# Two-problem grouped-query attention on one core: later wq pieces issued by ScalarE in another shape, first loads and x transposes in another order

## The chip, the cores and the metric

The kernel runs on one core of one Trainium2 chip. The metric is the device time of one execution in microseconds (us), the median of three runs. The engines are TensorE (PE in profiles; PEld is its weight load), VectorE (DVE), ScalarE (ACT), GpSimd (POOL) and SyncE (SP, which here only issues transfers). Transfers are issued on SyncE's queue or on ScalarE's queue and are carried out by 16 DMA engines.

## The reference

Two independent problems, A and B, of the same shapes; their outputs are set side by side. All data is bf16.

```python
B, Sq, D = 16, 80, 576
Hq, Hkv, Sk, Dh = 32, 16, 512, 128
q = (x @ wq).reshape(B, Sq, Hq, Dh).transpose(0, 2, 1, 3)
k = jnp.repeat(k_cache, Hq // Hkv, axis=1)
v = jnp.repeat(v_cache, Hq // Hkv, axis=1)
scores = jnp.einsum("bhqd,bhkd->bhqk", q, k) * (Dh ** -0.5)
p = softmax(scores, axis=-1)
o = jnp.einsum("bhqk,bhkd->bhqd", p, v)
out = o.transpose(0, 2, 1, 3).reshape(B, Sq, Hq * Dh) @ wo
# result: concatenate([out_A, out_B], axis=-1)
```

## The kernel before

**Units.** The attention is cut into 128 units U, 64 for each problem. A unit is one batch row and four K/V heads (eight query heads). Eight units in a row share one slice of wq (1024 columns, eight heads) and one half of the batch rows (8 rows of 80 queries); that group of eight is `goct`, 16 in all. For each pair of slices q the kernel goes through half 0 with both slices, then half 1 with both, so a slice is read by two `goct` (for instance 0 and 2). For each pair of slices there is then a share of the output projection.

**Work of a unit.** Four score tiles of 128 rows (one for each K/V head, 128 of its 160 query rows) and a fifth that packs the four rests of 32 rows. For a tile: QK on TensorE (L713, and L699 for the packed fifth, which takes two units at a time from the third unit on: `GRP`, `GR`); the negated row maximum on VectorE (L722); the exponential with its row sum on ScalarE (L726); a reciprocal on VectorE (L732); the scaling on GpSimd (L735); a transpose of P on TensorE (L741), copied out of PSUM by VectorE (L748, L750), or for some units' fifth tile by a DMA transpose (L754, units chosen by `RSEL`); P times V on TensorE (L788), copied out by ScalarE (L804). QK runs 13 tiles (`LA`) ahead of the rest.

**Projections.** `qp` (L589) multiplies xT by a slice of wq, for one head i of the slice and one half c of the eight rows; its result is scaled and copied to qT by ScalarE (L600) or VectorE (L601). `op` (L841) is the output projection, out of oT and wo. Problem A's x is loaded and transposed by TensorE (L507, copied out at L511); problem B's x comes by DMA transposes (`ldxt`, L527), five for each half.

**Loads.** K of a unit (L663, a DMA transpose into one of 5 slots) and x, wq, wo and the stores (L875) stand on SyncE's queue. V (L667) stands there for units 0 to 3 and on ScalarE's queue from unit 4 on. wq has two slots, one for even and one for odd slices. Slices 0 and 1 of problem A are loaded at the start, in two halves of 512 columns each (names w00, w01, w10, w11 in `FIRST`; x00 to x11 are x's parts, k0.. and v0.. the first K and V). Later slices (`goct` 4, 5, 8, 9, 12, 13) are loaded in four pieces and a rest of 64 rows (L560, L563).

**Order.** The program of every engine is an order worked out at build time by `_Sched.arrange`. Each operation has an engine (or a choice of engines), a stream, a key that sorts it within its stream, and a duration. At each step the planner takes the engine that can start first and gives it the operation of least key among the heads of its streams. Transfers get a landing time from a cost model (`dma_end`) or, for the first loads, from the table `LAND`. `after` holds a transfer back in the plan until a given P-times-V step; on the chip only real dependencies are waited for, by semaphores. Within a queue operations go in the planned order, and an operation that waits holds up what is behind it.

**What the change touches.** `FIRST`, `LATER` and `LAND` (order and landing of first loads); `WENG` (who issues later wq pieces), `WQR` and `WQX` (when: units after `sp_`, the start of the second pass of the projection that last reads the slot), `XR` (when each of the ten DMA transposes of x goes: first step and distance, in units, relative to the first projection that reads it, for half 0 and half 1); the wq pieces' shape at L556; the dependencies of `qp` on them at L607.

Of the kernel before, what the change touches and what calls it, by code (L numbers as in the profile page):

```python
# [13 lines left out]
LA = 13  # L14
# [9 lines left out]
VK = 8.0  # L24
KK = 8.0
DLAT = 0.6
XC = 0.4
QL2 = 10.3
VC = 1.75
WQC = 3.1  # L30
# [6 lines left out]
NWARM = 8  # L37
NWARM2 = 2
QP1 = (0.4, 1.1)
FIRST = ("x00", "w00", "x01", "w01", "k0", "w10", "k1", "v0", "k2", "k3", "v1", "w11", "k4")  # L40
LATER = dict(x10=-0.40, x11=-0.39, v2=-0.38, v3=-0.37)
LAND = dict(x00=4.1, w00=6.4, x01=8.0, w01=9.6, k0=11.5, w10=14.6, k1=18.1, v0=19.4, k2=21.8, k3=23.7, v1=26.4, w11=28.1,
            k4=30.3, k5=33.0, x10=35.7, x11=36.9, v2=38.0, v3=39.5, k6=43.2, k7=46.8)
NFK = 5
PTX = (0,)
NPX = 128
QEV = {160: dict(act=0.21, dve=0.24), 320: dict(act=0.32, dve=0.40), 480: dict(act=0.43, dve=0.57)}
NWC = 4
BANKS = dict(S=(0, 1, 2, 6), T=(3, 4), O=(5, 7), M=(7, 5), M0=(7, 5, 6, 3, 4), M1=(7, 6), ML=(7, 5, 6, 0, 1))
# [1 line left out]
VENG = "act"  # L51
VDUR = 0.42
VN = 1
# [6 lines left out]
XM = dict(wo=6.0, wq=6.0, wqb=6.0, RT=4.0, V=2.0, K=2.0, x=3.0)  # L60
VAF = (None, None, None, None)
STENG = "sp"
WENG = "sp"
WOENG = "sp"
WLAG = 2.0
NVS = 4
# [21 lines left out]
LPS = 1.1  # L88
LPC = 29.0
WOR = (((4.0, 1.5), (12.0, 1.5)), ((7.0, 1.6), (15.6, 1.6)), ((8.0, 1.7), (16.0, 1.7)), ((9.0, 1.7), (16.0, 1.4)))  # L90
WQR = (2.0,3.5,9.5)
WQX = {9: (5.0, 2.0), 13: (4.0, 2.0)}
XR = ((-12.0, 1.9), (-9.5, 1.6))

MM0 = 0.0025
MM1 = 1.0 / 2400.0
# [274 lines left out]
def bass_concat_heads__gqa_block_cached__gqa_block_cached__near_ridge_kernel(  # L371
# [27 lines left out]
    with ExitStack() as es:  # L399
# [6 lines left out]
        kT = sb("kT", [128, NK, 4, 512], BF16)  # L406
# [24 lines left out]
        S = _Sched()  # L431

        def R(res, ver):
            return (res, ver)
# [33 lines left out]
        def em_warmend(e):  # L468
# [5 lines left out]
              stream="warmset")  # L474
# [12 lines left out]
        for half in range(NPP):  # L487
            x_ap = probs[0][0]
            for part, (k0, k1) in enumerate(XP):
                def em_ldx(e, x_ap=x_ap, half=half, k0=k0, k1=k1):  # L490
                    src = x_ap.rearrange("b s d -> (b s) d")[half * NROW + k0 * 128:half * NROW + k1 * 128, :]
                    return e.dma_start(xs[:, half * NRT + k0:half * NRT + k1, 0:D],
                                       src.rearrange("(k p) d -> p k d", p=128))

                S.add("sp", FIRST.index("x%d%d" % (half, part)) - 100.0 if half == 0 else LATER["x%d%d" % (half, part)], em_ldx,
                      writes=[R(("xs", half * NRT + k_), 0) for k_ in range(k0, k1)], dsem="d_x%d%d" % (half, part), land=LAND["x%d%d" % (half, part)],
                      name="ldx%d.%d" % (half, part), stream="later" if half else "first", dur=0.5, cost=XC * (k1 - k0))
            for blk in range(NRT):
                rb = half * NRT + blk
                vb = S.bank("M0" if half == 0 else "M1")  # L500
                x = (XA + 0.5 * blk if blk < 2 else XA + XB + 0.1 * blk) if half == 0 else XH + 0.8 * blk

                def em_xtr(e, rb=rb, vb=vb):
                    last = None
                    for ck in range(5):
                        c0 = ck * 128 if ck < 4 else D - 128
                        last = e.transpose(psb[:, vb.phys, ck * 128:(ck + 1) * 128], xs[:, rb, c0:c0 + 128], ident[:])  # L507
                    return last

                def em_xev(e, en=None, half=half, blk=blk, vb=vb):  # L510
                    return (e.copy if en == "act" or half == 0 and blk in (1, 3) else e.tensor_copy)(xT[:, half, :, blk * 128:(blk + 1) * 128],  # L511
                                         psb[:, vb.phys, 0:640].rearrange("p (c n) -> p c n", c=5))

                S.add("pe", x, em_xtr, reads=[R(("xs", rb), 0), IDENT], writes=[R(vb, 0)], name="xtr%d" % rb,
                      stream="X", dur=_mm(5, 128), lat=0.2, alloc=[vb])
                S.add(("act", "dve") if half else "act" if blk in (1, 3) else "dve", x + 0.3, em_xev, reads=[R(vb, 0)], writes=[R(("xT", half, blk), 0)],
                      name="xev%d" % rb, stream="xed" if half else "xea" if rb in (1, 3) else "xev",
                      dur=dict(act=0.52, dve=0.40), lat=0.13)

        for half in range(NPP):  # L520
            x_ap = probs[1][0]
            st0 = UPR + 16 * half - lead[NG // 2 + 2 * half]
            for ck in range(5):
                def em_ldxt(e, x_ap=x_ap, half=half, ck=ck):
# [6 lines left out]
                      writes=[R(("xT", half, b_), 1) for b_ in range(NRT)] if ck == 0 else [R(("xT", half, "t", ck), 1)],  # L531
# [7 lines left out]
        for goct in range(NG):  # L539
            prob, q, half = unit(goct)  # L540
            wq_ap = probs[prob][3]
            wv = prob * NOCT + q
# [2 lines left out]
            pieces = () if half else ((0, 512), (512, 1024)) if goct < 2 else ((0, 1024),)  # L545
            for pi, (c0, c1) in enumerate(pieces):
                st0 = u0 - lead[goct]
                t_ld = 5.0 * st0 - 20.0 if goct > 1 else FIRST.index("w%d%d" % (goct, pi)) - 100.0
                dsem = "d_wq%d" % wsl
                eng = "sp" if goct < 2 else WENG  # L550
                strm = "first" if goct < 2 else "wq"
                sp_ = st0 if goct < 2 else u0 - 16 - lead[goct - 2] + max(QSH, lead[goct - 2] - QS0)
                if goct < 2:
                    parts = ((4, 5, c0, c1), (0, 4, c0, c1))
                else:
                    parts = tuple((0, 4, 256 * j, 256 * j + 256) for j in range(4)) + ((4, 5, 0, 1024),)  # L556
                for j, (k0, k1, n0, n1) in enumerate(parts):
                    def em_ldw(e, wq_ap=wq_ap, q=q, wsl=wsl, n0=n0, n1=n1, k0=k0, k1=k1):
                        if k0 == 4:
                            return e.dma_start(wq_sb[64:128, wsl, 4, n0:n1],  # L560
                                               wq_ap[512:576, q * 1024 + n0:q * 1024 + n1])
                        src = wq_ap[k0 * 128:k1 * 128, q * 1024 + n0:q * 1024 + n1]
                        return e.dma_start(wq_sb[:, wsl, k0:k1, n0:n1], src.rearrange("(c p) n -> p c n", p=128))  # L563

                    at = WQR[0] + WQR[1] * j + WQX.get(goct, (0.0, 0.0))[0] if k0 == 0 else WQR[2] + WQX.get(goct, (0.0, 0.0))[1]
                    S.add("act" if not goct + pi + j else eng, t_ld + 0.01 * j if goct < 2 else 5.0 * (sp_ + at), em_ldw,
                          writes=[R(("wq", wsl, k0 // 4, p_), wv) for p_ in range(n0 // 256, n1 // 256)],
                          dsem="d_we%d_%d_%d" % (goct, pi, j) if goct < 2 else "%s_%d" % (dsem, j),
                          name="ldw%d.%d.%d.%d" % (goct, pi, k0, n0), stream="wqa" if not goct + pi + j else strm if goct < 2 or k0 == 0 else "wqb", dur=0.5,
                          cost=(0.12 + 0.8 * WQC if k0 < 4 else 0.4) * (n1 - n0) / 1024.0 * (1.0 if goct < 2 or k0 else 1.25),  # L570
                          after=int(4 * (sp_ + at)) if goct > 1 else None,
                          lag=WLAG if goct > 1 else 0.0,
                          land=LAND["w%d%d" % (goct, pi)] if goct < 2 else 0.0)

            for i in range(8):
                for c in range(2):
# [77 lines left out]
        for U in range(NSU):  # L654
# [10 lines left out]
            def em_ldv(e, vc_ap=vc_ap, b=b, q=q, vs=vs):  # L665
                src = vc_ap[b:b + VN, 4 * q:4 * q + 4, :, :].rearrange("b g (p j) d -> p b g (j d)", j=4)
                return e.dma_start(v_sb[:, vs:vs + VN, :, :], src)  # L667

            S.add("sp", FIRST.index("k%d" % U) - 100.0 if U < NFK else 5.0 * gfirst[U] + 0.5 * (U - gfirst[U]) - LA - KK, em_ldk, writes=[R(("kT", ks), U)],
                  dsem="d_k%d" % ks, name="ldk%d" % U, stream="K" if U >= NFK else "first", dur=1.8, cost=KC, xp=True,  # L670
                  after=4 * U - KPH if U >= KU0 else None, lag=KLAG if U >= KU0 else 0.0, land=LAND.get("k%d" % U, 0.0))
            if U % VN == 0:
                S.add(VENG if U >= NVS else "sp", FIRST.index("v%d" % U) - 100.0 if U < 2 else LATER["v%d" % U] if U < NVS else 5.0 * U - VK, em_ldv, writes=[R(("V", vs + i_), U + i_) for i_ in range(VN)],
                      dsem="d_v%d" % vs, name="ldv%d" % U, stream="V" if U >= NVS else "later" if U > 1 else "first", dur=VDUR, cost=VN * VC,
                      lag=VLAG if U >= NVS else 0.0, after=VAF[U] if U < 4 else 4 * U - VPH if U >= VU0 else None,
                      land=LAND.get("v%d" % U, 0.0))

            vo = None
            rdma = any(a_ <= U < b_ and U % 4 in m_ for a_, b_, m_ in RSEL)
            for k in range(5):  # L680
# [274 lines left out]
```

## Time and profile before

| what | value |
|---|---|
| median of three runs | 765.19 us (764.51 to 765.31) |
| the profiled execution, its own time | 765.12 us |
| its span | 763.4 us |
| time around the span | 1.72 us |
| HBM read and written | 87.46 MB and 2.95 MB |
| DMA moved, mean | 172.86 MB, 226 GB/s |
| TensorE idle after 740 us, output projection's tail | 2.6 us of 23.4 |

The profile is of one execution. Its page begins with the busy time of each engine, then cuts the span in 40 equal slices (each digit is the busy share of a slice in tenths, 9 is 90% or more) and lists the DMA queues and the chain of work that ended last. The trace behind it answers finer questions: the timeline of one engine in a window, the busy time of all engines in a stretch, the issues of transfers with the time to landing. Ends of matmuls are modelled, so an interval between two starts says more than the idle time in brackets. "L713" is a line of the kernel; a letter q behind an engine (SPq, ACTq) marks the issuing of a transfer by it.

Transfers by issuing line, as the page has them: V on ScalarE's queue, 124 of 512 KB, 5.1 us from issue to landing; K on SyncE's queue, 128, 6.8 to 7.0 us; transposes of P, 94, 4.9 us; later wq pieces, 24 of 256 KB (5.0 to 5.2 us) and 6 of 128 KB, on SyncE's queue; wo, 32 of 288 KB; transposes of x, 10, 4.7 us.

### The profile page before, as it was taken

To read this page: it belongs to the slowest core of one execution; us is meant where nothing else is said; L and a number is where in the kernel's file an instruction comes from. 1 tells how busy PE (TensorE), PEld (TensorE's weight loads), DVE (VectorE), ACT (ScalarE), POOL (GpSimd) and SP (SyncE) were. 2 spreads that over 40 slices of the span, in tenths; PEclk is the share of its full clock that TensorE was granted. 3 is DMA by queue.
4 is the path that set the end of the run, shared out by engine and by line. 5 is a ranking of instruction groups with operands and counts; after the bars stand their busy time and mean duration, and the time that the engine had idled before them with its cause. 6 is when DMAs were issued, how large, how long until landed. Compare 5 with 4: busy or idle time off the path is not lost.

```text
span 763.4 us, 21017 instructions
## 1 busy us (share of the span) xinstructions
PE 756.6 (99%) x7876; PEld 572.3 (75%) x7876; DVE 676.7 (89%) x1602; ACT 603.7 (79%) x1691; POOL 432.3 (57%) x647
## 2 busy tenths in 40 slices
PE   8999999999999999999999999999999999999998
PEld 4677777777777777777777777777777777777786
DVE  5999999998888898999989999889889989999982
ACT  3878988888888887787887878887888888877860
POOL 1646755656565565565656555655656565564660
PEclk9999999999999999999999999999999999999999
DMA  9999999999998999999999999999999999999751
GB/s 223 261 244 240 244 248 262 233 222 234 196 240 198 255 258 251 261 218 210 241 228 214 226 248 247 240 251 251 234 219 214 199 227 237 226 264 258 182 121 32
DMA packets 431364, 172.86 MB, mean 226 GB/s; under 512 B 327968, under 2 KB 430880, under 8 KB 431264
## 3 DMA queue, kind: packets, MB, share of 16 engines
q1 hardware_dynamic: 365712, 106.43, 78.4%
q10 hardware_dynamic: 65552, 65.09, 28.4%
q8 instruction: 64, 1.05, 0.6%
q14 instruction: 36, 0.29, 0.1%
HBM read 87.46 MB, written 2.95 MB: 118 GB/s over the span
## 4 chain that ended last, share of the span: by engine, by line
PE 97%; DVE 1%; ACT 1%; issue 0%
PE ps L589 23%; PE ps L841 21%; PE ps L788 18%; PE ps L741 16%; PE ps L713 14%; PE ps L699 5%; DVE negmax L722 1%; PE ps L461 0%; ACT p_sb L726 0%; PE ps L507 0%; DVE qT L601 0%; DVE xT L511 0%; ACT qT L600 0%; ACT xT L511 0%; DVE pT L750 0%
## 5 line engine op out<-in xcount | busy, mean ns | idle before, releaser
L735 POOL TENSOR_SCALAR p_sb<-p_sb,rinv 128x512 bf16<-128x512 bf16 x640 | 429.9, 692 | 308.9 <-DVE rinv L732 308.8
L726 ACT ACTIVATE p_sb<-ps,negmax 128x512 bf16<-128x512 f32 x640 | 440.9, 695 | 90.8 <-DVE negmax L722 81.4
L722 DVE TENSOR_REDUCE negmax<-ps 128x1 f32<-128x512 f32 x640 | 425.1, 680 | 17.0 <-PE ps L713 12.2
L788 PE MATMUL ps<-pT,v_sb 128*128 128x160 bf16 x2048 | 221.9, 233 | 0.0
L750 DVE COPY pT<-ps 128x512 bf16<-128x512 bf16 x512 | 206.1, 414 | 11.9 <-PE ps L741 11.2
L589 PE MATMUL ps<-xT,wq_sb 128*128 128x320 bf16 (+2 forms) x1280 | 213.5, 299 | 1.6 <-ACT xT L511 0.7
L741 PE MATMUL ps<-ident,p_sb 128*128 128x128 bf16 x2184 | 209.8, 219 | 0.0
L788 PEld LDWEIGHTS ps<-pT,v_sb 128*128 128x128 bf16 x2048 | 164.6, 98 | 47.7 <-issue 2.1
L713 PE MATMUL ps<-kT,qT 128*128 128x512 bf16 x512 | 193.4, 379 | 0.0
L741 PEld LDWEIGHTS ps<-ident,p_sb 128*128 128x128 bf16 x2184 | 155.1, 98 | 34.4 <-issue 5.1
L841 PE MATMUL ps<-wo_sb,oT 128*128 128x288 bf16 x1280 | 170.0, 286 | 0.0
L589 PEld LDWEIGHTS ps<-xT,wq_sb 128*128 128x128 bf16 x1280 | 116.0, 98 | 52.7 <-DVE qT L601 2.5
L841 PEld LDWEIGHTS ps<-wo_sb,oT 128*128 128x128 bf16 x1280 | 122.4, 98 | 34.6 <-issue 1.7
L804 ACT CAST oT<-ps 128x320 bf16<-128x320 f32 x256 | 109.0, 426 | 29.5 <-PE ps L788 27.9
L726 ACT ACTIVATION_READ_ACCUMULATOR p_sb<-ps,negmax 128x1 f32 x640 | 132.1, 206 | 0.0
L601 DVE TENSOR_SCALAR qT<-ps 128x320 bf16<-128x320 f32 (+2 forms) x158 | 76.5, 485 | 13.8 <-PE ps L589 11.1
L600 ACT ACTIVATE qT<-ps 128x320 bf16<-128x320 f32 x98 | 43.1, 440 | 15.6 <-PE ps L589 15.4
L713 PEld LDWEIGHTS ps<-kT,qT 128*128 128x128 bf16 x512 | 50.0, 98 | 2.8 <-issue 0.2
L732 DVE RECIPROCAL rinv<-rowsum 128x1 f32<-128x1 f32 (+2 forms) x222 | 36.3, 165 | 8.2 <-ACT p_sb L726 8.2
L869 DVE TENSOR_TENSOR osb<-ps,acc 128x288 bf16<-128x288 f32 x40 | 18.3, 457 | 27.1 <-PE ps L841 27.1
L699 PE MATMUL ps<-kT,qT 128*32 128x512 bf16 x512 | 39.6, 384 | 1.0 <-ACT oT L804 0.6
L853 ACT COPY acc<-ps 128x288 f32<-128x288 f32 x40 | 15.9, 397 | 2.9 <-PE ps L841 2.7
(19 smaller groups left out, 46.3 us busy)
## 6 DMA issues: line engine op xcount, KB each, us to landing
v_sb<-in_B_v_cache_dram ACTq DMA_DIRECT2D x64, 512.0 KB, 5.1
v_sb<-in_A_v_cache_dram ACTq DMA_DIRECT2D x60, 512.0 KB, 5.1
wo_sb<-in_A_wo_dram SPq DMA_DIRECT2D x16, 288.0 KB, 5.3
wo_sb<-in_B_wo_dram SPq DMA_DIRECT2D x16, 288.0 KB, 4.6
wq_sb<-in_B_wq_dram SPq DMA_DIRECT2D x16, 256.0 KB, 5.2
out_dram<-osb SPq DMA_DIRECT2D x40, 72.0 KB, 3.4
wq_sb<-in_A_wq_dram SPq DMA_DIRECT2D x4, 512.0 KB, 5.1
v_sb<-in_A_v_cache_dram SPq DMA_DIRECT2D x4, 512.0 KB, 5.4
```

Of the source, the lines that this page charges most:

```text
L589: last = e.matmul(ps[:, vb.phys, 0:n1 - n0], lhsT=wq_sb[:, wsl, ck, i * 128:(i + 1) * 128], rhs=xT[:, half, ck, n0:n1], start=(ck == 0), s ...
L601: return e.tensor_scalar(dst, src, SCALE, None, op0=AluOpType.mult)
L699: last = e.matmul(ps[32 * g4:32 * g4 + 32, vb_.phys, :], lhsT=qT[:, qp_, g4 * 160 + 128:g4 * 160 + 160], rhs=kT[:, ks_, :, g4 * 128:(g4 + ...
L713: return e.matmul(ps[:, vb.phys, :], lhsT=qT[:, qp, gl * 160:gl * 160 + 128], rhs=kT[:, ks, :, gl * 128:(gl + 1) * 128], start=True, stop= ...
L722: return e.tensor_reduce(negmax[:, si:si + 1], ps[:, vb.phys, :], axis=AX.X, op=AluOpType.max, negate=True)
L726: return e.activation(p_sb[:, psl, :], ps[:, vb.phys, :], AF.Exp, bias=negmax[:, si:si + 1], scale=1.0, accum_out=rowsum[:, ss, k:k + 1])
L735: return e.tensor_scalar(p_sb[:, psl, :], p_sb[:, psl, :], rinv[:, ss, k:k + 1], 1.0, op0=AluOpType.mult, op1=AluOpType.mult)
L741: last = e.transpose(psb[:, vt.phys, j * 128:(j + 1) * 128], p_sb[:, psl, j * 128:(j + 1) * 128], ident[:])
L750: return cp(pT[:, pts, :, 0:4, gl * 32:gl * 32 + 32], psb[:, vt.phys, 0:512].rearrange("p (j h c) -> p j h c", j=4, h=4))
L788: last = e.matmul(ps[:, vo.phys, off:off + 160], lhsT=v_sb[:, vs, gl, j * 128:(j + 1) * 128], rhs=pT[:, pts, j, :, gl * 32:gl * 32 + 32], ...
L804: return e.copy(dst, src)
L841: last = e.matmul(ps[:, vb.phys, 0:DC], lhsT=oT[:, hi, rb * 128:(rb + 1) * 128], rhs=wo_sb[:, hi, c3 * DC:(c3 + 1) * DC], start=(hi == 0), ...
```

## The change

The second half of the second wq slice (w11) leaves its place ahead of K 4 and goes behind K 4, K 5, V 2 and x's second half; V 2 goes ahead of x. These loads now form one stream with the first ones. The later wq pieces, and their rest of 64 rows, are issued by ScalarE. A piece has 256 rows and 512 columns instead of 512 rows and 256 columns, its time in units after `sp_` is 5, 7, 10, 12.5 and, for the rest, 9.5 (before 2, 5.5, 9, 12.5 and 9.5), and the extra delays for `goct` 9 go, while those for `goct` 13 become 2 and 2. A projection depends on both pieces of its columns and on the rest. The DMA transposes of x are 1.7 units apart for half 0 (before 1.9) and, for half 1, begin 12 units ahead instead of 9.5. `NPY = 0` makes the new option `PTY` empty, so the copies of transposed P are chosen as before. The planner's landing and cost figures change.

```diff
-FIRST = ("x00", "w00", "x01", "w01", "k0", "w10", "k1", "v0", "k2", "k3", "v1", "w11", "k4")
-LATER = dict(x10=-0.40, x11=-0.39, v2=-0.38, v3=-0.37)
-LAND = dict(x00=4.1, w00=6.4, x01=8.0, w01=9.6, k0=11.5, w10=14.6, k1=18.1, v0=19.4, k2=21.8, k3=23.7, v1=26.4, w11=28.1,
-            k4=30.3, k5=33.0, x10=35.7, x11=36.9, v2=38.0, v3=39.5, k6=43.2, k7=46.8)
+FIRST = ("x00", "w00", "x01", "w01", "k0", "w10", "k1", "v0", "k2", "k3", "v1", "k4")
+LATER = ("v2", "x10", "x11", "w11", "v3")
+FKEY = dict([(n_, i_ - 100.0) for i_, n_ in enumerate(FIRST)] + [(n_, 0.05 * i_ - 0.49) for i_, n_ in enumerate(LATER)])
+LAND = dict(x00=4.1, w00=6.4, x01=8.0, w01=9.6, k0=11.5, w10=14.5, k1=18.0, v0=19.3, k2=21.8, k3=23.7, v1=26.4, k4=28.7,
+            k5=31.4, v2=33.2, x10=34.4, x11=36.0, w11=37.7, v3=39.4, k6=43.2, k7=46.5)
...
-NPX = 128
+PTY = (1,)
+NPY = 0
...
-WENG = "sp"
+WENG = "act"
...
-WQR = (2.0,3.5,9.5)
-WQX = {9: (5.0, 2.0), 13: (4.0, 2.0)}
-XR = ((-12.0, 1.9), (-9.5, 1.6))
+WQR = (5.0, 7.0, 10.0, 12.5, 9.5)
+WQX = {13: (2.0, 2.0)}
+XR = ((-12.0, 1.7), (-12.0, 1.6))
...
-                    parts = tuple((0, 4, 256 * j, 256 * j + 256) for j in range(4)) + ((4, 5, 0, 1024),)
+                    parts = tuple((2 * (j % 2), 2 * (j % 2) + 2, 512 * (j // 2), 512 * (j // 2) + 512) for j in range(4)) + ((4, 5, 0, 1024),)
...
-                    at = WQR[0] + WQR[1] * j + WQX.get(goct, (0.0, 0.0))[0] if k0 == 0 else WQR[2] + WQX.get(goct, (0.0, 0.0))[1]
+                    at = WQR[j] + WQX.get(goct, (0.0, 0.0))[k0 // 4]
...
-                          writes=[R(("wq", wsl, k0 // 4, p_), wv) for p_ in range(n0 // 256, n1 // 256)],
+                          writes=[R(("wq", wsl, w_, p_), wv) for w_ in range(k0 // 2, (k1 + 1) // 2) for p_ in range(n0 // 256, n1 // 256)],
...
-                          name="ldw%d.%d.%d.%d" % (goct, pi, k0, n0), stream="wqa" if not goct + pi + j else strm if goct < 2 or k0 == 0 else "wqb", dur=0.5,
-                          cost=(0.12 + 0.8 * WQC if k0 < 4 else 0.4) * (n1 - n0) / 1024.0 * (1.0 if goct < 2 or k0 else 1.25),
+                          name="ldw%d.%d.%d.%d" % (goct, pi, k0, n0), stream="wqa" if not goct + pi + j else strm if goct < 2 or k0 < 4 else "wqb", dur=0.5,
+                          cost=((0.12 + 0.8 * WQC) * (k1 - k0) / 4.0 if k0 < 4 else 0.4) * (n1 - n0) / 1024.0 * (1.0 if goct < 2 or k0 == 4 else 1.1),
...
-                          reads=[R(("wq", wsl, w_, i // 2), wv) for w_ in range(2)] + [R(("wqz",), 0)] + xr,
+                          reads=[R(("wq", wsl, w_, i // 2), wv) for w_ in range(3)] + [R(("wqz",), 0)] + xr,
...
-                    free_ = k in PTX and U < NPX
+                    free_ = k in PTX or k in PTY and U < NPY
```

The remaining lines of the diff replace the old look-ups in `FIRST` and `LATER` by `FKEY`, and put all first loads of SyncE into one stream ("first").

More of the change, by code (lines that the diff above doesn't have):

```diff
@@ L493, in em_ldx @@
                                        src.rearrange("(k p) d -> p k d", p=128))
-                S.add("sp", FIRST.index("x%d%d" % (half, part)) - 100.0 if half == 0 else LATER["x%d%d" % (half, part)], em_ldx,
+                S.add("sp", FKEY["x%d%d" % (half, part)], em_ldx,
                       writes=[R(("xs", half * NRT + k_), 0) for k_ in range(k0, k1)], dsem="d_x%d%d" % (half, part), land=LAND["x%d%d" % (half, part)],
-                      name="ldx%d.%d" % (half, part), stream="later" if half else "first", dur=0.5, cost=XC * (k1 - k0))
+                      name="ldx%d.%d" % (half, part), stream="first", dur=0.5, cost=XC * (k1 - k0))
             for blk in range(NRT):
@@ L547, in bass_concat_heads__gqa_block_cached__gqa_block_cached__near_ridge_kernel @@
                 st0 = u0 - lead[goct]
-                t_ld = 5.0 * st0 - 20.0 if goct > 1 else FIRST.index("w%d%d" % (goct, pi)) - 100.0
+                t_ld = 5.0 * st0 - 20.0 if goct > 1 else FKEY["w%d%d" % (goct, pi)]
                 dsem = "d_wq%d" % wsl
@@ L667, in em_ldv @@
                 return e.dma_start(v_sb[:, vs:vs + VN, :, :], src)
-            S.add("sp", FIRST.index("k%d" % U) - 100.0 if U < NFK else 5.0 * gfirst[U] + 0.5 * (U - gfirst[U]) - LA - KK, em_ldk, writes=[R(("kT", ks), U)],
+            S.add("sp", FKEY["k%d" % U] if U < NFK else 5.0 * gfirst[U] + 0.5 * (U - gfirst[U]) - LA - KK, em_ldk, writes=[R(("kT", ks), U)],
                   dsem="d_k%d" % ks, name="ldk%d" % U, stream="K" if U >= NFK else "first", dur=1.8, cost=KC, xp=True,
@@ L672, in bass_concat_heads__gqa_block_cached__gqa_block_cached__near_ridge_kernel @@
             if U % VN == 0:
-                S.add(VENG if U >= NVS else "sp", FIRST.index("v%d" % U) - 100.0 if U < 2 else LATER["v%d" % U] if U < NVS else 5.0 * U - VK, em_ldv, writes=[R(("V", vs + i_), U + i_) for i_ in range(VN)],
-                      dsem="d_v%d" % vs, name="ldv%d" % U, stream="V" if U >= NVS else "later" if U > 1 else "first", dur=VDUR, cost=VN * VC,
+                S.add(VENG if U >= NVS else "sp", FKEY["v%d" % U] if U < NVS else 5.0 * U - VK, em_ldv, writes=[R(("V", vs + i_), U + i_) for i_ in range(VN)],
+                      dsem="d_v%d" % vs, name="ldv%d" % U, stream="V" if U >= NVS else "first", dur=VDUR, cost=VN * VC,
                       lag=VLAG if U >= NVS else 0.0, after=VAF[U] if U < 4 else 4 * U - VPH if U >= VU0 else None,
```

## The prediction

> **What bounds the kernel now.** First the page's first two parts, for the share of each engine and how evenly it lies over the span.
>
> ```profile
> span 763.4 us, 21017 instructions
> PE 756.6 (99%) x7876; PEld 572.3 (75%) x7876; DVE 676.7 (89%) x1602; ACT 603.7 (79%) x1691; POOL 432.3 (57%) x647
> PE   8999999999999999999999999999999999999998
> PEclk9999999999999999999999999999999999999999
> DMA  9999999999998999999999999999999999999751
> q1 hardware_dynamic: 365712, 106.43, 78.4%
> q10 hardware_dynamic: 65552, 65.09, 28.4%
> PE 97%; DVE 1%; ACT 1%; issue 0%
> ```
>
> TensorE is busy in every slice at the full granted clock and makes 97% of the chain that ended last. The change alters no matmul, transpose or eviction in number or size. So it can win only what TensorE loses between its instructions, and it can lose without such a limit. DMA is also full: its two queues (q1 is SyncE's, q10 ScalarE's) together make 106.8% of the engines' time, which is more than 100% because packets of both overlap. Transfers that are late are therefore the place to look.
>
> Next, TensorE's own timeline at the two places where it lost most after the first 15 us:
>
> ```profile
> 32.58 0.44 PE L788 MATMUL ps<-pT,v_sb 128*128 128x160 bf16 x4
> 33.60 0.61 PE L699 MATMUL ps<-kT,qT 128*32 128x512 bf16 x8 [0.59 <-ACT oT L804]
> ...
> 406.90 0.84 PE L589 MATMUL ps<-xT,wq_sb 128*128 128x320 bf16 x5
> 408.12 0.61 PE L699 MATMUL ps<-kT,qT 128*32 128x512 bf16 x8 [0.38 <-issue]
> ```
>
> Columns: start, us, what runs, and in brackets the idle time before it. Four matmuls of L788 issue in 0.28 us elsewhere (34.38 to 34.66), so TensorE was free at 32.86 and lost 0.74 before 33.60. Five of L589 issue in 0.68 (403.58 to 404.26), so it was free at 407.58 and lost 0.54 before 408.12, of which about 0.1 is lost before many groups of L699. Both waiting groups are the packed QK of two steps (L699). The page names ScalarE or nothing, but both need a fresh K, and its transposes stand on SyncE's queue (issues by line, in a narrow window about each):
>
> ```profile
> v_sb<-in_A_v_cache_dram SPq DMA_DIRECT2D x1, 512.0 KB, 4.9
> wq_sb<-in_A_wq_dram SPq DMA_DIRECT2D x1, 512.0 KB, 5.5
> kT<-in_A_k_cache_dram SPq DMA_TRANSPOSE x1, 7.2
> kT<-in_A_k_cache_dram SPq DMA_TRANSPOSE x1, 5.6
> kT<-in_B_k_cache_dram SPq DMA_TRANSPOSE x1, 8.8
> ```
>
> The last number is us from issue to landing. In order: V 1 (issued 21.57, lands 26.5), the second half of the second wq slice (22.75, 28.2), K 4 (23.38, 30.6), K 5 (27.92, 33.52) and K 71 (399.28, 408.04). K 5 and K 71 land 0.08 us before TensorE starts. These are the two late transfers. After 15 us, K 1 (1.4 us to spare), K 3 (0.25), V 2 (0.48) and K 7 (0.82) are near it; every other K, V or transposed P lands 1.7 us or more ahead of its reader, most 5 to 15.
>
> I sorted TensorE's start-to-start times by the pair of neighbouring instructions and took what each exceeds the usual of its pair by. That gives 9.2 us in all: 2.6 before 15 us, 2.6 from there to 41 us (0.74 is K 5; then 0.43 at 25.74 and 0.31 and 0.27 at 36.76 and 38.12, which wait for evictions by VectorE), 0.45 at K 71, and 3.5 in crumbs of at most 0.1. The realistic most that a better order of loads can win is 0.74 + 0.43 + 0.31 + 0.27 + 0.45 = 2.2 us.
>
> **The change part by part.**
>
> *Second half of the second wq slice behind K 4, K 5, V 2 and x.* It lands 28.2 - 26.5 = 1.7 us behind V 1 and everything after it on the queue waits that long. Taken out, K 4 lands near 28.9 and K 5 near 31.8. V 2 now goes ahead of x: 31.8 + 2.0 = 33.8 instead of 37.4. x lands within 0.4 us of before, the half slice near 37.4, V 3 as before. Its cover: its first reader starts at 43.77, so 6.4 us stay where 15.6 were; without that cover each us late would be a us of projections late. The stall before K 5 is bounded by 0 and 0.74. For 0.74: the other thing that group waits for, a bank freed by an exponential that ended at 32.77, is ready. For 0: VectorE is full there.
>
> ```profile
> 20.00:45.00 25.00, 23.85 (x244) 16.59 (x242) 24.76 (x56) 22.55 (x64) 15.74 (x24) 1.00 1.15 252
> ```
>
> This is the table of stages (us, then busy PE, PEld, DVE, ACT, POOL): VectorE 24.76 of 25. TensorE resumed earlier will meet unfinished maxima and evictions, and give some of the 0.74 back. I take 0.5, as the wait is on data that comes 1.7 us sooner and ScalarE has 2.4 us free.
>
> *Second x (the five transposes for half 1 of problem B) 2.5 units earlier.* A unit is one batch row of four head groups, 5 score tiles, about 5.85 us, so each issues near 14.6 us earlier (356.7 becomes about 342, 398.1 about 383). Five transposes of 1.2 us issue time move; x for half 0 moves by at most 0.8 unit. Readers start at 411.59, so nothing waits for them. What they leave is SyncE's queue before K 71:
>
> ```profile
> 383.40 5.24 SPq L663 DMA_TRANSPOSE kT<-in_B_k_cache_dram  x1
> 388.74 1.21 SPq L754 DMA_TRANSPOSE pT<-p_sb  x1
> 390.00 0.58 SPq L875 DMA_DIRECT2D out_dram<-osb  x1
> 390.62 1.16 SPq L527 DMA_TRANSPOSE xT<-in_B_x_dram  x1
> 391.82 4.26 SPq L663 DMA_TRANSPOSE kT<-in_B_k_cache_dram  x1
> 396.18 1.21 SPq L754 DMA_TRANSPOSE pT<-p_sb  x1
> ```
>
> Back to back: the queue runs behind. Between 383 and 399, two x transposes leave (2.3 us of issue), and the wq piece at 380.16 moves to about 352. K 71 needs to be only 0.45 sooner. I take the whole 0.45; bounds 0 and 0.54.
>
> *Later wq pieces: 30 issues move from SyncE to ScalarE* (six slices, four pieces and a 64-row rest each). On SyncE each takes 0.58 us, so 17 us leave a queue that has idle time except in such backlogs: already counted above. On ScalarE the 124 V loads show the price: 0.37 to 0.40 us each, 30 x 0.40 = 12 us over the span at most. But they run beside its work:
>
> ```profile
> 84.67 0.45 ACT L600 ACTIVATE qT<-ps 128x320 bf16<-128x320 f32 x1
> 84.80 0.37 ACTq L667 DMA_DIRECT2D v_sb<-in_A_v_cache_dram  x1
> 84.98 0.71 ACT L726 ACTIVATE p_sb<-ps,negmax 128x512 bf16<-128x512 f32 x1
> ```
>
> The issue starts inside one activation and the next starts before it ends. I take 0. Cover gone, it is 0.4 to 0.58 of ScalarE for each piece, and banks that its exponentials free come that much later. ScalarE is busiest at 80 to 100 us (19.2 of 20), where about two pieces go: a bound of 1.2 us. Their waits (earlier readers of the slot) are met: the first piece now goes 5 units after the old slice's last pass begins, when the four heads it overwrites are 1 unit past, so nothing queues behind a blocked issue. Arrival: pieces of 512 columns mean that the first projection needs two pieces instead of one; the second is due about 11 units in, near 93 us for a reader at 126 us. On every slice more than 15 us remain.
>
> *512-column pieces.* 512 B rows become 1 KB rows: 12,288 packets of 35.0 ns become 6,144 of 54.4 (both means from the trace's packets by size; the second is V's). Over 16 engines 26.9 us become 20.9. It is 0.8% of the span on the DMA engines, hidden wherever TensorE waits for no transfer, so 0, and it helps K 71. As for the other queue, the two queues' shares (78.4 and 28.4%) already overlap in one set of engines. [...]
>
> *The rest* (cost and landing figures, the planner's dependencies, an option with limit 0) issues nothing. It does re-lay the order by hand of all engines, which can shift crumbs either way: 0, bounds -0.5 and +0.5.
>
> **Sum**, from the profiled execution's 765.12 (span 763.4 and 1.72 around it; the median is 765.19): 765.12 - 0.5 - 0.45 = 764.17, about **764.2**, range of its own 763.4 to 764.9.
>
> **Rivals.**
> 1. *The start gains more.* With V 2 and K 5 early, the new order also fills the gaps at 25.74, 36.76 and 38.12. For: the V 2 wait (37.43 landed, 37.91 read) goes. Against: those gaps wait for VectorE, which is full. All 2.2 won gives 762.9; two thirds, 763.3 as its value.
> 2. *Nothing is won.* VectorE gives K 5's time back, and SyncE's backlog, which starts near 360 us where every unit's transposed P goes by DMA, still holds K 71. 765.1.
> 3. *Slower: the backlog moves forward to 345 to 395 us.* The x transposes now lie among K 61 to K 69 while the wq pieces, on the other queue, take turns with K in the same engines instead of standing behind it. K 69 lands 4.0 us before its reader, K 67 7.3, and the backlog before was about 4 to 5 us. It decides from the point where the queue is 4 us later than now at 383 us: K 69, 71 and 73 then each hold TensorE by about 1 us: 765.12 - 0.5 + 3 = 767.6. Added to it in the bad case are ScalarE's 1.2 us of pieces. Against: the same bytes in fewer packets and four issues fewer on SyncE there.
> 4. *The change does not do what it says* has little room: loads are issued in the order written; a K 5 ahead of V 2 depends on the planner, which before put K 5 ahead of x. It falls under 2.
>
> **How the numbers follow.** Chances: forecast 0.42, more at the start 0.23, nothing 0.10, slower 0.25. A measurement of this kernel tells about 0.2%, 1.5 us, from no change: faster is below 763.66, slower above 766.72. Faster: all but a little of rival 1 and a quarter of the forecast, 0.22 + 0.10 = 0.32. Slower: most of rival 3, 0.24. Within: 0.44. The range leaves out 1 in 10 at each end: low 762.9 is all of the 2.2 won, high 767.2 cuts the upper half of rival 3.
>
> **What would show it.** K 5 landing near 31.8, and no gap over 0.3 us before the packed QK near 33; no gap near 408, with K 71 landing a us or more before its reader; ScalarE's issues of wq_sb at 0.4 us beside activations, with its waits for maxima not longer; wq packets of 1 KB on q10; TensorE busy 10.00 of 10 us after 45. I am wrong if TensorE shows new gaps at 345 to 430 us (rival 3), at 80 to 125 us beside wq issues (ScalarE), or the same sum of gaps before 41 us (rival 2).

## The result and the profile after

The changed kernel took 771.10 us, median of 20 runs (765.33 to 778.54), beside 765.31 us for the kernel before on the same occasion (20 runs, 764.35 to 768.88). The ratio is 1.0059, 95% interval 1.0036 to 1.0081, some 4.5 us. (Ratios, here and below, leave out runs more than 1.5% above the fastest of their kernel; medians, ranges and counts take in every run.) So it is slower, but not by a steady amount: its fastest run equals the median of before, and 13 of its 20 runs lie above 768 us, where before has 3.

The profiled execution is one of the longer ones: 775.4 us, span 773.7 us, 10.3 us more than before. Its page, the parts that answer to those of before:

```profile
span 773.7 us, 21014 instructions
PE 761.0 (98%) x7876; PEld 574.8 (74%) x7876; DVE 679.0 (88%) x1611; ACT 603.1 (78%) x1682; POOL 432.4 (56%) x647
q1 hardware_dynamic: 352560, 99.36, 78.1%
q10 hardware_dynamic: 72560, 72.17, 33.0%
PE 91%; DVE 5%; DMA 2%; ACT 1%; issue 1%; ACTq 0%
kT<-in_A_k_cache_dram SPq DMA_TRANSPOSE x64, 8.1
kT<-in_B_k_cache_dram SPq DMA_TRANSPOSE x64, 7.8
```

The work is the same (7876 matmuls). wq's 7 MB have moved from q1 (SyncE's queue) to q10 (ScalarE's). K, whose transposes stayed where they were, now takes 7.8 to 8.1 us from issue to landing instead of 6.8 to 7.0. ScalarE's own busy time has not grown (603.1 for 603.7), and the chain of work that ended last now has DMA in it.

The planner's order gives each TensorE instruction a planned start. In the trace of before, TensorE runs 0.2 us ahead of that at the end; in this one it ends 10.2 us behind. Nearly all of the 10 us comes in five steps: 0.7 us at 48.0 (K 7), 1.0 at 386 to 398 (K 67, a transposed P, K 69), 4.2 at 537 to 545 (K 93 and a transposed P), 0.6 at 706.7 (a transposed P) and 4.4 at 711 to 719 (K 123). TensorE's timeline at the third step:

```profile
538.00 0.61 PE L701 MATMUL ps<-kT,qT 128*32 128x512 bf16 x8 [0.17 <-issue]
538.55 0.40 PE L743 MATMUL ps<-ident,p_sb 128*128 128x128 bf16 x4
541.22 0.69 PE L790 MATMUL ps<-pT,v_sb 128*128 128x160 bf16 x4 [2.28 <-issue]
541.71 0.63 PE L743 MATMUL ps<-ident,p_sb 128*128 128x128 bf16 x4
```

At 541.22 it had waited 2.3 us, for a transposed P that landed at 541.13: planned for 524.33, it was issued at 531.04, behind K 93 on SyncE's queue, and was then 10.1 us in flight. But look at the durations after the gap: 0.63 us for the four transposes that took 0.40 before it. The table of stages shows why (us, busy PE, PEld, DVE, ACT, POOL, then the granted clock, DMA share, GB/s):

```profile
520.00:537.00 17.00, 17.00 (x176) 13.00 (x175) 15.48 (x38) 13.62 (x37) 9.93 (x15) 1.00 1.27 194
537.00:545.00 8.00, 5.55 (x46) 3.71 (x45) 4.82 (x12) 3.38 (x11) 3.70 (x7) 0.79 1.28 228
711.00:719.00 8.00, 5.30 (x47) 3.79 (x45) 4.35 (x11) 3.28 (x9) 3.04 (x5) 0.79 1.02 250
719.00:740.00 21.00, 21.00 (x235) 16.49 (x232) 19.52 (x46) 17.11 (x49) 12.64 (x20) 1.00 0.90 203
```

At the end of each of the two long gaps the granted clock is half for 3.41 us (0.79 is the mean of the 8 us), which adds some 1.7 us to each (an estimate, half of the 3.41). The third step cost 4.2 us, of which TensorE waited 2.5 for the late transfer. The idle times ahead of the two stretches were 2.28 and 2.70 us; what makes the clock halve, no run shows.

Who was late? The issues of K 93, K 123 and K 7, each in a narrow window:

```profile
kT<-in_B_k_cache_dram SPq DMA_TRANSPOSE x1, 14.9
kT<-in_B_k_cache_dram SPq DMA_TRANSPOSE x1, 13.7
kT<-in_A_k_cache_dram SPq DMA_TRANSPOSE x1, 8.7
```

14.9 and 13.7 us where 7 is usual: these two K were not issued impossibly late (3.0 and 9.2 us behind plan), they were long in flight. Packets were slow in both stretches: the 95th percentile of the 1 KB packets on ScalarE's queue, by stretches of 20 us, is 229 ns at 520 to 540 and 224 to 229 at 680 to 720 us, and 46 to 68 in half of the stretches. Beside K 93 two wq pieces and a 64-row rest were in flight; beside K 123, with nearly half of the loss, none, only V.

Finally the start. The gap before K 5 is gone (the packed QK at 33.06, K 5 landed at 30.35), and a new one stands at the next pair of units:

```profile
46.48 0.84 PE L591 MATMUL ps<-xT,wq_sb 128*128 128x320 bf16 x5
47.97 0.61 PE L701 MATMUL ps<-kT,qT 128*32 128x512 bf16 x8 [0.65 <-issue]
```

K 7 was issued at 39.13 and landed at 47.88, 0.09 us before; in the kernel before, issued at 39.59, it had landed at 46.25. Beside it flies V 5, which ScalarE now issues at 39.93 instead of 43.54. The gap lost 0.72 us, K 5's had lost 0.74.

### The profile page after: what moved, and what is told of

Read it like the earlier page. It is cut to its first block, busy times and chain, and to the rows that moved or that the text cites. A ratio compares the mean times of both kernels' runs of the same rounds, so it can differ in the third digit from the quotient of the medians.

```text
span 773.7 us, 21014 instructions
## 1 busy us (share of the span) xinstructions
PE 761.0 (98%) x7876; PEld 574.8 (74%) x7876; DVE 679.0 (88%) x1611; ACT 603.1 (78%) x1682; POOL 432.4 (56%) x647
## 4 chain that ended last, share of the span: by engine, by line
PE 91%; DVE 5%; DMA 2%; ACT 1%; issue 1%; ACTq 0%
PE ps L591 21%; PE ps L843 20%; PE ps L790 17%; PE ps L743 14%; PE ps L715 13%; PE ps L701 4%; DVE negmax L724 3%; DMA pT<-p_sb 2%; DVE pT L752 1%; ACT p_sb L728 1%; DVE qT L603 1%; PE ps L463 0%; PE ps L509 0%; ACT xT L513 0%; DVE pT L750 0%
## 5 line engine op out<-in xcount | busy, mean ns | idle before, releaser
L701 PEld LDWEIGHTS ps<-kT,qT 128*32 128x32 bf16 x512 | 8.0, 94 | 15.1 <-issue 6.7
```

The lines of the kernel that those rows point to most:

```text
L701: last = e.matmul(ps[32 * g4:32 * g4 + 32, vb_.phys, :], lhsT=qT[:, qp_, g4 * 160 + 128:g4 * 160 + 160], rhs=kT[:, ks_, :, g4 * 128:(g4 + ...
```

## The experiments

Theory I (issuer): on a second queue wq's packets run against those of the K and P transposes, instead of standing in line with them. Rivals: the pieces' shape, times and x steps (T, later split in P, packet size, B, bunching, and X, the x steps), the start order (S), ScalarE's issuing time (E), and the chips themselves (C). Each kernel was timed in five rounds; kernels of one group ran on one chip beside the kernel before.

### First group: the parts of the change

**e1**: the changed kernel, with

```diff
-WENG = "act"
+WENG = "sp"
```

> The changed kernel with its later wq pieces issued by SyncE again; their shape, their times, the x steps and the start order stay changed. Theory I (issuer): wq on ScalarE's queue takes turns with the K and P transposes in the same 16 DMA engines, K lands late, TensorE stands still for some 2.5 us and its granted clock then halves for 3.41 us. It expects 763 to 765.5 us, granted clock 1.000 in nearly every run, and K latency back at 6.5 to 7.5 us. Theory T (shape, times and x steps overload the DMA engines whoever issues): 768 to 774 us with clocks of 0.993 to 0.998. Theory S (start order): the same 768 to 774.

**e2**: the kernel before with the start order (and its landing figures) alone:

```diff
-FIRST = ("x00", "w00", "x01", "w01", "k0", "w10", "k1", "v0", "k2", "k3", "v1", "w11", "k4")
+FIRST = ("x00", "w00", "x01", "w01", "k0", "w10", "k1", "v0", "k2", "k3", "v1", "k4")
+LATER = ("v2", "x10", "x11", "w11", "v3")
```

> The kernel before with the new start order and its landing figures alone. Theories I and T: 764 to 765 us, the gap before K 5 gone or shifted, clock 1.000. Theory S (the start order sets the lateness off): 768 to 774 us.

**e3**: the kernel before with

```diff
-WENG = "sp"
+WENG = "act"
```

> The kernel before with its later wq pieces, in their old shape (512 rows by 256 columns) and at their old times, issued by ScalarE. Theory I: slower, 767 to 774 us, spread over several us, clocks under 1.000 in many runs, K latency 8 us or more in the stretches with wq pieces. Theory T: 764.5 to 766.5 us, clock 1.000. Theory S: as T.

**e4**: the changed kernel with the start order of before (the reverse of e2's diff).

> The changed kernel with the start order and landing figures of before; wq on ScalarE's queue, new shape, times and x steps. Theory I and theory T: still 768 to 774 us with clocks under 1.000. Theory S: 764 to 766 us, clock 1.000.

| kernel | wq issued by | median, us | range | runs above 768 | ratio to before |
|---|---|---|---|---|---|
| before | SyncE | 765.62 | 764.53 to 774.30 | 7 of 33 | |
| e1 | SyncE | 766.23 | 764.64 to 773.55 | 3 of 12 | 1.0011 [0.9980, 1.0041] |
| e2 | SyncE | 766.53 | 764.70 to 773.54 | 4 of 12 | 1.0018 [0.9989, 1.0047] |
| e3 | ScalarE | 767.46 | 765.59 to 773.72 | 5 of 12 | 1.0013 [0.9983, 1.0043] |
| e4 | ScalarE | 776.31 | 765.30 to 786.86 | 9 of 10 | 1.0054 [1.0012, 1.0096] |

Theory S falls for most of the loss: without the new start order the change is as slow as with it (e4). T by itself falls: with shape, times and x steps left changed, wq back on SyncE's queue is near before (e1). I is borne out in part. In the changed kernel the issuer makes the difference (e1 beside e4, which has the old start order as well: 3 of 12 runs above 768 us beside 9 of 10); but every kernel, that of before too, has some long runs, and e3, the issuer in the kernel before, is not told apart from it. So the issuer is needed for the loss; that it is enough by itself is not shown. e1 also misses what theory I gave it: 766.23 for 763 to 765.5, with the clock at 1.000 in 7 of 12 runs, not in nearly all.

### Second group: shape, times, x, and how full DMA is

**g1**: the changed kernel with pieces in the old shape. The planned order of all compute engines is the changed kernel's (one figure of the planner's cost model for wq differs too).

```diff
-                    parts = tuple((2 * (j % 2), 2 * (j % 2) + 2, 512 * (j // 2), 512 * (j // 2) + 512) for j in range(4)) + ((4, 5, 0, 1024),)
+                    parts = tuple((0, 4, 256 * j, 256 * j + 256) for j in range(4)) + ((4, 5, 0, 1024),)
```

> The changed kernel with its later wq pieces in the old shape (512 rows by 256 columns, rows of 512 B), at the changed times, issued by ScalarE; the planned order of every engine's work is the same as in the changed kernel. Theory P (issuer and packet size: in each DMA engine a 1 KB packet of the second queue takes about twice the time of a 512 B one between two 256 B packets of K): median 766 to 769 us, near the 767.5 of old shape and old times on ScalarE, and K latency with a piece in flight under 8.7 us. Theory B (issuer and bunching: the changed times put pieces 2 to 3 units apart and two slices' pieces together): 770 to 777 us as the changed kernel, K latency 9 us or more.

**g2**:

```diff
-WQR = (5.0, 7.0, 10.0, 12.5, 9.5)
-WQX = {13: (2.0, 2.0)}
+WQR = (5.0, 8.5, 12.0, 15.5, 9.5)
+WQX = {9: (2.0, 2.0), 13: (1.0, 2.0)}
```

> The changed kernel with its pieces (new shape, ScalarE) spaced evenly by 3.5 units as before the change, from 5 units on. Theory P: still 769 to 777 us, clocks under 1.000 in half the runs or more. Theory B: 765.5 to 768 us.

**g3**:

```diff
-XR = ((-12.0, 1.7), (-12.0, 1.6))
+XR = ((-12.0, 1.9), (-9.5, 1.6))
```

> The changed kernel with the DMA transposes of x at the steps of before. Theories P and B: 769 to 777 us as the changed kernel, since x moves only at 250 to 285 and 340 to 400 us. Theory X (the earlier x transposes set the lateness off): 765 to 767 us.

**g4**: in all 17 entries of `RSEL`, the units whose fifth P tile a DMA transposes:

```diff
-(0, 1, 2, 3)
+(0, 1, 2)
```

> The changed kernel with 68 instead of 94 transposes of P done by DMA; TensorE does the other 26, at 4 x 0.055 us each some 5.7 us more work (planned end 6.1 us later). All theories of a full set of DMA engines (P, B, X): 769.5 to 772 us in nearly all runs, spread under 3 us, clock 1.000, K latency under 8 us. Theory E (ScalarE is late with its own work because it issues 30 transfers more, and DMA is not the cause): the spread stays, 771 to 783 us with clocks of 0.993 to 0.998.

| kernel | median, us | range | runs above 768 | ratio to before |
|---|---|---|---|---|
| before | 765.84 | 764.48 to 771.59 | 9 of 29 | |
| g1 | 769.00 | 765.19 to 780.53 | 6 of 12 | 1.0014 [0.9984, 1.0044] |
| g2 | 773.29 | 765.43 to 789.65 | 10 of 12 | 1.0054 [1.0019, 1.0089] |
| g3 | 776.32 | 771.62 to 787.18 | 6 of 6 | 1.0109 [1.0065, 1.0154] |
| g4 | 771.45 | 770.48 to 773.44 | 12 of 12 | 1.0060 [1.0040, 1.0080] |

g4 is the clearest. With 26 DMA transposes fewer, TensorE has the extra work, so the floor rises, but the spread falls from over 13 us to 3.0, and the granted clock is 1.000 in every run. ScalarE still issues all 30 pieces, so E falls. 26 transposes fewer relieve the DMA engines and SyncE's queue at once; which of the two ends the long runs, g4 does not tell. Its page:

```profile
span 770.4 us, 21218 instructions
PE 763.2 (99%) x7980; PEld 578.7 (75%) x7980; DVE 682.1 (89%) x1600; ACT 608.0 (79%) x1693; POOL 432.4 (56%) x647
q1 hardware_dynamic: 338416, 95.94, 72.0%
q10 hardware_dynamic: 72560, 72.17, 32.8%
```

The two queues' shares together are 104.8% here, 111.1% in the changed kernel's trace and 106.8% in that of before. B falls (g2, even spacing, is no better), X too (g3, in six runs). g1 is within P's range, but its range overlaps that of the changed kernel. P took a 1 KB packet for about twice the time of a 512 B one; the packet records of the kernel before have 54.4 ns for 35.0.

### Third group: shape again, smaller packets, one queue

**h1** is the changed kernel and **h2** is g1, both again.

> The changed kernel once more, on the chip of the following three. Theory I with P: median 769 to 776 us, more than half of the runs over 768 us.

> The changed kernel with its pieces in the old shape (512 B rows) at the changed times on ScalarE's queue, once more. Theory P (packet size matters besides the issuer): median 2 us or more under the changed kernel of the same chip, a third to a half of the runs over 768 us. Issuer alone: the same median within 1.5 us.

**h3**: smaller pieces (with dependencies by 128 columns, four more semaphores for each slot, and another cost figure in the planner)

```diff
-                    parts = tuple((2 * (j % 2), 2 * (j % 2) + 2, 512 * (j // 2), 512 * (j // 2) + 512) for j in range(4)) + ((4, 5, 0, 1024),)
+                    parts = tuple((0, 4, 128 * j, 128 * j + 128) for j in range(8)) + ((4, 5, 0, 1024),)
...
+WQR = (5.0, 6.0, 7.0, 8.0, 10.0, 11.25, 12.5, 13.75, 9.5)
```

> The changed kernel with each later slice in eight pieces of 512 rows by 128 columns (256 B rows) on ScalarE's queue, spread over the changed times: 54 issues instead of 30. Theory P: packets as small as K's share the engines evenly, K never stands still for a piece; median 765.5 to 768.5 us, K latency with a piece in flight 8 us or less. Theory Q (what counts is the time that wq takes of the full DMA engines, and 24,576 packets of 256 B take about 37 us of the 16 engines instead of 21): 772 to 780 us.

**h4**: e1, and V too on SyncE's queue:

```diff
-VENG = "act"
-WENG = "act"
+VENG = "sp"
+WENG = "sp"
```

> The changed kernel with both the later wq pieces and all of V issued by SyncE, so that no second queue is left. Theory I: K's transposes never stand still for a burst of another queue; K latency near 6.5 us with little spread and 763.5 to 765.5 us, clock 1.000 in all runs, if SyncE's 124 more issues of 0.58 us find room. Against: SyncE's issue of a K blocks its queue for 2 to 8 us, V stands behind it with 4.5 to 11 us to spare, and comes late: 768 us or more, with V as what the late groups of P times V wait for.

| kernel | median, us | range | runs above 768 | ratio to before |
|---|---|---|---|---|
| before | 767.08 | 764.55 to 778.63 | 9 of 23 | |
| h1 | 772.27 | 765.42 to 780.56 | 8 of 12 | 1.0058 [1.0021, 1.0096] |
| h2 | 770.09 | 765.33 to 781.48 | 9 of 12 | 1.0038 [1.0009, 1.0068] |
| h3 | 774.93 | 769.59 to 788.14 | 6 of 6 | 1.0098 [1.0067, 1.0129] |
| h4 | 814.27 | 808.68 to 817.82 | 6 of 6 | 1.0612 [1.0578, 1.0647] |

P falls as an explanation of the time: the smallest packets (h3) bring no gain, and their median is within Q's range (Q: what counts is how long wq occupies the DMA engines), though the intervals of h3 and h1 overlap. Old and new shape are not told apart (h2 and h1, 2.2 us with overlapping intervals). h4 fails for the reason given against it; TensorE waits for V, in the worst place for 4.34 us:

```profile
318.85 0.69 PE L790 MATMUL ps<-pT,v_sb 128*128 128x160 bf16 x4 [4.34 <-DMA v_sb<-in_A_v_cache_dram]
```

But with no second queue K is 6.1 to 6.3 us in flight in the median, where I had said near 6.5, the shortest of all kernels.

```profile
kT<-in_A_k_cache_dram SPq DMA_TRANSPOSE x64, 6.3
kT<-in_B_k_cache_dram SPq DMA_TRANSPOSE x64, 6.1
```

### Fourth and fifth group: the issuer alone, and what the rest is worth

What was open: the changed kernel with either issuer and nothing else altered had not been timed on one chip, and chips may differ. **j1** is the changed kernel, **j2** is e1, **j3** has the last three of the six slices on SyncE's queue:

```diff
-                eng = "sp" if goct < 2 else WENG
+                eng = "sp" if goct < 2 or goct > 8 else WENG
```

> The changed kernel, on one chip with the next two. Theory I (issuer): median 769 us or more, over half of the runs above 768 us.

> The changed kernel with its later wq pieces on SyncE's queue and nothing else altered. Theory I: median 764.7 to 767 us, a third of the runs or fewer above 768 us, and 3 us or more under the changed kernel on this chip. Theory C (the chips differ, the issuer does not matter): within 1.5 us of the changed kernel.

> The changed kernel with the last three of its six later slices (from 300 us on) on SyncE's queue, the first three on ScalarE's. Theory I: a median between those of the other two. Theory C: as both.

**k1** is e1 again, **k2** is e1 with the start order of before.

> The changed kernel with its later wq pieces on SyncE's queue, a third time. If the rest of the change is worth what was forecast (K 5 and K 71, 0.95 us): a ratio of 0.9985 or less and runs at 763.6 to 764.2 us. If not: the fastest runs at 764.5 as before, ratio within 0.002 of 1.

> The same with the start order and landing figures of before. If the new start order gains 0.5 us: slower than the other of this chip by that. If the wait only goes from K 5 to K 7: the same fastest runs within 0.2 us.

| kernel | median, us | range | runs above 768 | ratio to before |
|---|---|---|---|---|
| before (beside j) | 765.99 | 764.38 to 772.64 | 5 of 29 | |
| j1 | 768.89 | 764.61 to 782.93 | 6 of 12 | 1.0026 [1.0000, 1.0052] |
| j2 | 765.02 | 764.61 to 767.78 | 0 of 12 | 0.9990 [0.9975, 1.0005] |
| j3 | 770.03 | 765.53 to 774.20 | 7 of 12 | 1.0031 [1.0002, 1.0060] |
| before (beside k) | 767.01 | 764.66 to 779.61 | 6 of 23 | |
| k1 | 766.26 | 764.36 to 781.21 | 5 of 12 | 1.0006 [0.9978, 1.0035] |
| k2 | 765.59 | 764.53 to 779.14 | 5 of 12 | 1.0018 [0.9989, 1.0049] |

On one chip, with one setting altered, the issuing queue is worth 3.9 us in the median of all runs and 2.8 by the ratios (j1, j2; the intervals overlap a little; 6 and 0 of 12 runs lie above 768 us, of which some is luck, as k1, the same kernel as j2, has 5). C falls; j1 itself is just under the 769 us, and the more than half of its runs, that theory I gave it. The setting also lets the planner lay the work out anew: in the traces ten copies go from VectorE to ScalarE, and at 474 of TensorE's 7876 places in order stands another kind of matmul. The planned end is 0.7 us sooner (762.87 for 763.60); so the new order by itself explains 0.7 us by plan, and whether it makes K late less often was not tried. j3 does not lie between: the first three slices on ScalarE's queue are as bad as all six, so a dose was not shown. Over all occasions, 27 of 44 runs of the changed kernel lie above 768 us, 8 of 36 with wq on SyncE's queue (e1, j2, k1; with k2, 13 of 48) and 39 of 157 of the kernel before. No version beats both kernels: with wq on SyncE's queue the rest of the change equals before (the fastest runs at 764.4 to 764.6), with either start order.

j1's profiled execution has the longest wait on record, 7.6 us for K 51, which was 18.5 us in flight beside a wq piece, a 64-row rest and three V, in a stretch of slow packets again (95th percentile 224 ns at 280 to 300 us):

```profile
300.71 1.05 PE L701 MATMUL ps<-kT,qT 128*32 128x512 bf16 x8 [7.62 <-issue]
...
kT<-in_A_k_cache_dram SPq DMA_TRANSPOSE x1, 18.5
```

### What a burst on the other queue does to K

From the records of packets in the traces, by half us from 2.5 us after the issue of a K to 1.5 us before its landing: how many 256 B packets (K's and P's) started on SyncE's queue, by how many 1 KB packets ScalarE's queue started in the same half us (1 to 59 left out):

| 1 KB packets of ScalarE's queue in 0.5 us | none | 60 to 139 | 140 and more |
|---|---|---|---|
| changed kernel: 256 B packets, mean (median) | 337 (409) | 153 (142) | 16 (0) |
| changed kernel: such half us in all | 367 | 154 | 119 |
| before: 256 B packets, mean (median) | 343 (430) | 157 (150) | 15 (0) |
| before: such half us in all | 372 | 62 | 83 |
| j2: such half us in all | 373 | 69 | 84 |
| h1, the changed kernel in a run of 767.1 us: such half us in all | 370 | 89 | 116 |

While ScalarE's queue starts 140 packets and more in 0.5 us, K all but stands still (16 packets in the mean, 337 without), and this is so before the change too, with V (15 for 343). What the change adds is more such time: 273 half us (60 packets and more) instead of 145. Part of that is the long execution itself; h1 has 205. The mean flight of a K that has a wq piece in flight beside it is 7.84 to 9.62 us in the ten traces of the ScalarE kernels with all DMA transposes (the changed kernel 8.97, e3, e4, g1 to g3, h1 to h3, j1), and 7.26 to 7.98 in the six with wq on SyncE's queue (before 7.28, e1, e2, j2, k1, k2). A K without a piece beside it takes 6.7 to 7.4 us in the ten and 6.7 to 7.0 in the six. So a piece on the other queue costs a K more than one in line with it; that the latter delays K only once is a reading that fits, not shown by itself. Nor does the mean flight alone make the time: the lowest of the ten, 7.84, is h3's, whose median is no lower.

Slow packets are the other part, whoever issues wq: the 95th percentile reaches 215 to 224 ns in j2 too (80 to 100 and 200 to 220 us), and there, after 15 us, TensorE waits nowhere for more than 0.6 us but for K 7. The gaps of 2.28 us and more that are not before K 7 (two in the changed kernel, one each in g3 and j1; h4's wait for V aside) lie in, or right behind, a stretch of 20 us whose 95th percentile is 224 ns or more. That wq on ScalarE's queue delays K and slow packets make it worse is the account that fits; no run separates the two.

Whether the packets of two queues take turns one by one in a DMA engine, as P supposed, and why K gets so small a share beside a burst, these records do not show.

## Why the prediction was wrong

**What failed** is the step on the later wq pieces, "I take 0". It priced ScalarE's issuing time and the pieces' own arrival. Both were right: the issue takes 0.38 us beside the exponential (below), and no piece was late. But it gave the change of queue itself no price: the two queues' shares "already overlap in one set of engines", and so K was to share them with wq at no loss, which no run shows. What the runs showed in its place: with a piece in flight beside it, a K takes 7.84 to 9.62 us where the piece is on ScalarE's queue and 7.26 to 7.98 where it is on its own, and while that other queue starts 140 packets and more in 0.5 us, 16 packets start on K's in the mean, for 337 without. Taking wq off ScalarE's queue again was worth 2.8 to 3.9 us (j1, j2). That is rival 3's case, K held up by wq on the other queue, which had 0.25.

```profile
536.48 0.69 ACT L728 ACTIVATE p_sb<-ps,negmax 128x512 bf16<-128x512 f32 x1
536.48 0.38 ACTq L565 DMA_DIRECT2D wq_sb<-in_B_wq_dram  x1
```

**Rival 3's place and price.** It expected the backlog at 345 to 395 us. There the queue was 6.7 us later than before (K 69 issued at 390.13 for 383.40), past the 4 us that it named (the x transposes left it 7 to 12 us sooner, not 14.6, so the last two still lay ahead of K 68 and K 69), but K 67, a transposed P and K 69 cost some 1 us in all, not 3. Most was lost elsewhere, at K 93 and K 123, and at a price that I had not: a late K was taken as a us for a us, while the gaps of 2.28 and 2.70 us each came with 3.41 us at half clock as well, some 1.7 us on top. That, and waits longer than the 1 us it allowed for a K, made the range too short: its upper end, 767.2, is below the 771.1 measured.

**The spread.** Costing one execution gave no sign that the kernel before stands near an edge. Its trace had 1.7 us to spare in most places, but 25% of its later runs lie above 768 us, where the three runs shown ranged over 0.8 us.

**K 5.** The transfers came as worked out or sooner (K 4 at 28.1, K 5 at 30.4, V 2 at 32.8, the half slice at 36.7; forecast 28.9, 31.8, 33.8, 37.4) and the gap went. The gain did not: the step failed to say what is late next. TensorE came to the next pair of units earlier, V 5 on ScalarE's queue was issued earlier with it, and K 7, beside V 5, landed 1.6 us later. The 0.5 us were 0 (0.74 lost before, 0.72 after; the fastest runs of k1 and k2 are within 0.2 us). VectorE, which I named as the likely taker, was not what took it. The new order can also lose: TensorE waits 0.65 to 3.00 us for K 7 in all 14 traces that have it with V on ScalarE's queue, and less than that in the four with the old order; in e1 and h3 (2.68 and 3.00) the clock halved as well.

**K 71.** Right where ScalarE's queue does not spoil it: in j2 the packed QK at 408.07 follows with no gap. Its 0.45 us did not show in the fastest runs, as 1.25 us are lost before K 7 in that trace.

```profile
407.30 0.84 PE L591 MATMUL ps<-xT,wq_sb 128*128 128x320 bf16 x5
408.07 0.61 PE L701 MATMUL ps<-kT,qT 128*32 128x512 bf16 x8
```

**Packets.** 512 B rows gone, 1 KB rows on q10: as said, and of no use to the time. Rival 1's "two thirds" of 2.2 us would be 763.7, not 763.3; the range does not rest on it. "Nothing is won" (rival 2) holds for all of the change but the issuer.

**Open.** What makes packets slow in some stretches, and whether chips differ, was not settled. K 123 was late with no wq piece in flight, behind a queue that was already 9.2 us late, TensorE itself 5.2; whether that was still wq's doing is not known. Nor is it known whether the shape has a small part of its own, which of shape, times and x steps the issuer needs beside it (e3 has none of them), nor why half of the slices did as much as all.

## What to carry to other kernels

Where DMA engines are as full as here (two queues' shares of 106.8 and 111.1% together), the queue of a transfer is part of its price: with a wq piece in flight beside it K took 8.97 us in the changed kernel, where the piece is on the other queue, and 7.28 before, where it is on K's own. Try to keep transfers with time to spare behind those without, on the same queue (as long as its issues find room, which h4's did not), and price a move to another queue by what it takes from the late ones, not by its issue. Price a gap on TensorE like those of 2.28 us and more here with the 3.41 to 6.83 us at half clock that came with them (gaps of up to 1.82 us had none). And time a full kernel in many runs, for an edge shows in the spread before it shows in the median.

## What the runs showed of the hardware that was not expected

- A burst of 1 KB packets on ScalarE's queue (140 or more in 0.5 us) leaves the DMA transposes on SyncE's queue a median of 0 packets of 256 B in that time, 16 in the mean, where they have 337 without it.
- Gaps of 2.28 to 3.00 us on an otherwise full TensorE each came with 3.41 us at half the granted clock (two in the changed kernel, one each in e1 and h3), gaps of 3.87 to 7.62 us (g3, h4, j1) with 6.83 us. Gaps of 0.6 to 1.82 us, some 50 after 15 us in the 19 traces, did not.
- All loads on one queue gave K its shortest flight (6.1 to 6.3 us) and the slowest kernel (814 us).
